# Wo ahead of the next PV, and the second norm's pieces at once, in every chunk that is needed next

## The chip, the cores and the metric

The kernel runs on one core of a Trainium2 chip. The metric is device time in microseconds, the median of several executions. A profile of one more execution shows each engine: TensorE (PE, with its weight loads PEld), VectorE (DVE), ScalarE (ACT), GpSimd (POOL) and SyncE (SP), which here only issues transfers.

## The reference, cut to what matters

A transformer block for 2048 positions of width 1024: a layer norm, attention of 32 query heads on one shared key and value head of width 32, a residual, a second layer norm, a gated feed-forward part of width 3584, and a second residual.

```python
q = heads(norm(x) @ wq); k = norm(x) @ wk; v = norm(x) @ wv
o = softmax(q @ k.T * Dh**-0.5) @ v
h = x + merge(o) @ wo
h2 = h + (sigmoid(norm(h) @ w_gate) * (norm(h) @ w_up)) @ w_down
```

## The kernel before

**Tiling.** The 2048 positions are cut into 8 chunks of 256 queries (c = 0 to 7), each of two tiles of 128 positions (tt = 0, 1). The 32 heads are 8 quads of four heads (q = 0 to 7). For one chunk and one quad, attention goes through the keys in 8 bursts. A burst of scores (`s_burst`, line 637) is eight small matmuls into PSUM tile S_ps, two exponentials on ScalarE follow (`one_exp`, line 660) and write the ring `Pr`, and later the PV group of the quad multiplies them with V (line 754). The row sums of the softmax are added in pairs on VectorE (`add_pair`, lines 694 and 703) and finished by a few matmuls (line 734) inside the PV group. When a PV group ends, VectorE copies the bank out (lines 772 and 773), takes the reciprocal (778, 780) and multiplies (784); that gives the quad's attention output in `QT`.

**After attention of a chunk.** `wo_group` (four a chunk: two tiles by two halves of the width, eight matmuls of 512 columns each, recorded at line 316) multiplies by Wo; line 844 adds x. `stats2` makes the second norm: statistics of each half (line 866), their merge (870), a square root and reciprocal by powers on GpSimd (342, 344), the norm itself (`ln_norm`, line 348); `transpose2` has SP transpose the tile by a transfer (line 487). Only then can the chunk's feed-forward part begin: 14 pairs of gate and up groups (line 932, 16 matmuls of 256 columns each, with a tanh at 951 and a product at 971), then four down groups (line 996, 28 matmuls of 512 columns each), each ended by an add on VectorE (1006) and a store by SP.

**What sets the order.** The order of all instructions on all engines is made when the program is built, by a loop near the end of the function that keeps a clock for each engine with a cost for each instruction. TensorE has two PSUM banks (X_ps) for everything but scores; a group holds one from its first matmul until VectorE or ScalarE has emptied it. At each step the loop does the first of these that it can: a score burst, if ScalarE has freed its place and the ring has room (`ring_need`, line 605: the next burst needs the exponentials of nine bursts before to have been read by PV); an item of the open PV group, or, while its exponentials or sums are not there, of the current other group; an item of a group that is marked `first`; a new PV group, if all its bursts and one more have been issued; else an item of the current group, or a new group. `next_group` takes a Wo group if one is ready, else the head of `ffn_list`, where the groups of gate, up and down stand in the order of the chunks. A gate group is only taken once both transposes of its chunk have landed by the clocks.

A Wo group is marked `first` in chunk 0 alone. There its four groups run through before a new PV group is opened, and the statistics are issued directly behind each add. In the other chunks the pieces of the second norm are put at the end of `lo`, the list of VectorE work that fills the time up to the next dated instruction, behind the pair sums that stand there.

With `first` unset, a PV group that becomes ready is opened between two Wo groups.

Of the kernel before, what the change touches and what calls it, by code (L numbers as in the profile page):

```python
# [52 lines left out]
def when(*ticks):  # L53

    return max([0.0] + [t[0].time(t[1]) + 0.05 for t in ticks if t is not None])


def need(eng, *ticks):
    clk = CLK[id(eng)]
    for t in ticks:  # L60
        if t is not None and t[0].emit is not None and t[1] > t[0].n:
            t[0].emit(t[1])
    clk[0] = max(clk[0], when(*ticks))
    for t in ticks:
        if t is not None:
            t[0].wait(eng, t[1])
# [18 lines left out]
def bass_sequential_preLN__grouped_kv_mqa__glu_gated_glu__prompt_kernel(  # L85
# [18 lines left out]
    NQ = D // P  # L104
    QC = 256
    NQC = S // QC
    TPQ = QC // P
# [7 lines left out]
    RP = 18  # L115
    HR = 5
    NGU = 4
    G_SUM, NPB, NO_SUM = 3, 4, (NQ,)
    HG = 3
    WD_AT, WD_GAP, WD_LATE = 6, 6, 6  # L120
# [5 lines left out]
    with ExitStack() as es:  # L126
        EC = es.enter_context

        def sb(name, shape, dt=BF16):
            return EC(nc.sbuf_tensor(name, [P] + shape, dt))  # L130
# [9 lines left out]
        hact_flat = sb("hact", [NFT * QC])  # L140
        gu = sb("gu", [NGU, 512], F32)
        wgu = sb("wgu", [4, DT, 256])
# [78 lines left out]
        def _(unused):  # L221
# [108 lines left out]
            def ln_mean(i):  # L330
                return c_pool.inc(pool.tensor_copy(out=mean[:, i:i + 1], in_=mv[:, i:i + 1, 0]), 0.2)  # L331
# [384 lines left out]
            def pv_group(g):  # L716
                c, q = g // NQ, g % NQ
# [51 lines left out]
                def evac(bank, tick):  # L769
                    force("a", lambda: g < 1 or g - 1 in ols_read)  # L770
                    need(dve, tick, ols_read.get(g - 1))
                    dve.tensor_copy(out=ols[:, 0:QC], in_=bank[:, 0:QC])  # L772
                    free = c_dve.inc(dve.transpose(ols[:, QC:2 * QC], bank[:, QC:2 * QC]), 0.7, 0.08)  # L773
                    t_ = [None]

                    def recip():
                        need(dve, free)
                        r_ = c_dve.inc(dve.reciprocal(l8[:], ols[:, QC:2 * QC].rearrange("p (a b) -> p a b", b=32)[:, :, 0]), 0.23)
                        need(dve, r_)
                        t_[0] = c_dve.inc(dve.transpose(ols[:, QC:2 * QC], l8[:].unsqueeze(2).to_broadcast([P, QC // 32, 32])), 0.4)  # L780

                    def mult():
                        need(dve, t_[0])
                        ot_val[(c, q)] = ols_read[g] = c_dve.inc(dve.tensor_tensor(
                            out=QT[:, q, c * QC:(c + 1) * QC], in0=ols[:, 0:QC], in1=ols[:, QC:2 * QC],
                            op=ALU.mult), 0.4)
                    if g == NQ - 1:
                        force("a", lambda: not any(x[0] == "a" for x in lo))
                        recip()
                        mult()  # L790
                    else:
                        put("a", 0.65, recip, lambda: when(free))
                        put("a", 0.4, mult, lambda: when(t_[0]))
                    return free
# [5 lines left out]
            def put(chain, cost, fn, ready, first=False):  # L800
                n = 0 if first else len(lo)
                while n < len(lo) and lo[n][0][0] == "l":
                    n += 1
                lo.insert(n, (chain, cost, fn, ready))
# [17 lines left out]
            def force(chain, done):  # L822
                while not done():
                    if lo[0][0][0] == "l":
                        t = lo[0][3]()
                        if t is not None and t <= k_dve[0] + 0.1:
                            lo.pop(0)[2]()
                            continue
                    i = [j for j, x in enumerate(lo) if x[0] == chain][0]
                    lo.pop(i)[2]()  # L830
# [7 lines left out]
            def wo_group(c, tt, dc):  # L838
                t = c * TPQ + tt

                def evac(bank, tick):
                    need(dve, tick, hx_val[t])
                    hv = hx[:, t % HR, dc * 512:(dc + 1) * 512]
                    h_val[t] = c_dve.inc(dve.tensor_tensor(out=hv, in0=bank, in1=hv, op=ALU.add), 0.61, 0.08)  # L844
                    stats2(c, tt, dc)
                    if dc == DC - 1:
                        h_done.add(t)
                    return h_val[t]
                items = mm_list([(QT[:, q, c * QC + tt * P:c * QC + (tt + 1) * P], wo[:, q, dc * 512:(dc + 1) * 512])
                                 for q in range(NQ)], lambda bank: bank, 512)  # L850
                g = _Group(items, evac, [wo_val[0]] + [ot_val[(c, q)] for q in range(NQ)])
                g.first = c == 0
                return g

            ln2_pow = {}

            def stats2(c, tt, dc):
                t, first = c * TPQ + tt, c == 0
                idx = NT + t
                src = hx[:, t % HR, :]  # L860
                chain = "l%d" % (t % 2)
                h_tick = h_val[t]

                def part(cc):
                    need(dve, h_tick)
                    ins = dve.bn_stats(st[:, idx % 4, cc, :], src[:, cc * 512:(cc + 1) * 512])  # L866
                    k_dve[0] += 0.64
                    if cc == DC - 1:
                        need(dve, c_dve.inc(ins))
                        st2_val[t] = c_dve.inc(dve.bn_aggr(mv[:, idx, :], st[:, idx % 4, :, :]), 0.2)  # L870
                        if first:
                            need(dve, st2_val[t])
                            v = c_dve.inc(dve.tensor_scalar(out=vz[:, idx:idx + 1], in0=mv[:, idx:idx + 1, 1], scalar1=EPS_B,
                                                            scalar2=None, op0=ALU.add), 0.1)
                            ln2_pow[t] = ln_pow(idx, v)
                            ln_mean(idx)
                            ln2_pow[t] = (c_pool, c_pool.n)
                        else:
                            ln2_pow[t] = ln_rstd(idx, st2_val[t])

                def norm():
                    before = hn_read[t - TPQ] if c > 0 else xnT_read[NT - TPQ + tt]
                    hn_val[t] = ln_norm(src, hn[:, tt, :], idx, st2_val[t], ln2_pow[t], before)
                    transpose2(c, tt)
                if first:
                    part(dc)
                else:
                    put(chain, 0.85 if dc else 0.64, lambda: part(dc), lambda: when(h_tick))
                if dc == DC - 1:
                    put(chain, 0.5, norm, lambda: None if t not in ln2_pow or c > 0 and t - TPQ not in hn_read else  # L890
                        when(ln2_pow[t]), first)
# [52 lines left out]
            def gate_group(c, fp):  # L944
                n = c * NFP + fp
                slot = gu[:, n % NGU, :]

                def evac(bank, tick):
                    def tanh():
                        need(act, tick, gu_read.get(n - NGU))  # L950
                        tanh_val[n] = c_act.inc(act.activation(out=slot, in_=bank, func=ACTF.Tanh, scale=0.5), T_TANH, 0.1)  # L951

                    def free(must):
                        if must:
                            while n not in tanh_val:
                                act_one(act_next()[1])
                        return (tanh_val[n] if must else when(tanh_val[n]) if n in tanh_val else
                                max(k_act[0], when(tick)) + T_TANH + 0.2)
                    act_work.append((tick, tanh, lambda: when(tick, gu_read.get(n - NGU))))
                    return free  # L960
                return _Group(half_group(c, fp, 0, None, ()).items, evac, [hnT_val[c * TPQ + i] for i in range(TPQ)])

            def up_group(c, fp):
                n = c * NFP + fp
                slot = gu[:, n % NGU, :]

# [54 lines left out]
            q_list = collections.deque()  # L1021
            wo_list = collections.deque((c, tt, dc) for c in range(NQC) for tt in range(TPQ) for dc in range(DC))
            ffn_list = collections.deque()
# [7 lines left out]
            cur, pv = [None], [None]  # L1031

            def busy(g):
                return g is not None and bool(g.items)

            def wo_ready():
                if not wo_list:
                    return False
                c, tt, dc = wo_list[0]
                t = c * TPQ + tt  # L1040
                return t in hx_val and when(hx_val[t]) <= k_pe[0] and all(
                    (c, q) in ot_val and when(ot_val[(c, q)]) <= k_pe[0] for q in range(NQ))
# [85 lines left out]
            for p in range(1, BPG):  # L1128
# [11 lines left out]
                q = p + 2  # L1140
# [45 lines left out]
            while True:  # L1186
# [41 lines left out]
                if starved and busy(cur[0]):  # L1228
                    run_item(cur[0])
                    continue  # L1230
                if not busy(cur[0]) and wo_list and wo_list[0][0] == 0 and wo_ready():
                    cur[0] = next_group()
                if busy(cur[0]) and cur[0].first:
                    run_item(cur[0])
# [61 lines left out]
```

## Time and profile before

| | us |
|---|---|
| median of 3 runs (1132.32 to 1133.71) | 1132.54 |
| the profiled execution | 1132.68 |
| its span, first to last instruction | 1130.9 |
| TensorE busy | 1090.1 |
| ScalarE busy | 1006.6 |
| VectorE busy | 860.1 |

The page gives the busy time of each engine, then slices of a fortieth of the span whose digits are tenths busy. A timeline row gives start, duration, engine, line, operation, tile written and read, and in brackets the idle time just before and what ended it. A stage row gives the stretch, its length, and for each engine the busy time with the number of instructions in brackets, then the granted TensorE clock, the share of the DMA engines and GB/s. A few per cent of the matmul records are missing from the trace; the weight loads are all there (3584 of gate and up, 896 of down, 256 of Wo), so counts are taken from them.

### The profile page before, as it was taken

How to read it: one execution, taken by the hardware profiler on the slowest of the kernel's cores; microseconds unless marked ns; L12 is line 12 of the kernel's file. 1: busy time of each engine (PE TensorE's matmuls, PEld its weight loads, DVE VectorE, ACT ScalarE, POOL GpSimd, SP SyncE). 2: the span in 40 equal slices, each digit the busy share in tenths (PEclk: the TensorE clock that was granted, in tenths of full speed). 3: DMA queues.
4: the chain of work that ended last, by engine and by line, in shares of the span. 5: the costliest groups of instructions: out<-in, count | busy, mean ns of one | idle time of the engine just before them, and what ended most of it. 6: DMA issues, size and time to landing. Idle time of an engine off the chain costs nothing.

```text
span 1130.9 us, 33101 instructions
## 1 busy us (share of the span) xinstructions
PE 1090.1 (96%) x14332; PEld 660.1 (58%) x14395; DVE 860.1 (76%) x1538; ACT 1006.6 (89%) x1150; POOL 67.4 (6%) x142
## 2 busy tenths in 40 slices
PE   7999999999899999999899999999899989999998
PEld 5663447754476545764477545764377535775784
DVE  7769977778878798788887798878887788884111
ACT  6999999999999999999999999999999999990110
POOL 4410010000100000000000010000100010001000
PEclk9999999999999999999999999999999999999999
DMA  8834117860366415661266514662167522769600
GB/s 196 176 81 171 39 39 220 231 187 24 88 187 191 118 29 150 192 191 47 61 194 195 147 31 134 193 192 57 34 185 213 160 39 62 209 193 263 180 1 19
DMA packets 282065, 150.38 MB, mean 133 GB/s; under 512 B 38592, under 2 KB 276160, under 8 KB 281920
## 3 DMA queue, kind: packets, MB, share of 16 engines
q1 hardware_dynamic: 274144, 137.65, 45.2%
q0 software_dynamic: 2544, 9.44, 2.4%
q8 instruction: 113, 1.85, 0.7%
q10 hardware_dynamic: 5232, 1.18, 0.7%
q14 instruction: 32, 0.26, 0.1%
HBM read 136.18 MB, written 4.19 MB: 124 GB/s over the span
## 4 chain that ended last, share of the span: by engine, by line
PE 71%; ACT 11%; DVE 11%; issue 4%; POOL 2%; DMA 1%; DVEq 0%; ACTq 0%
PE X_ps L932 34%; PE X_ps L996 12%; PE S_ps L637 10%; ACT Pr L660 9%; PE X_ps L754 8%; PE X_ps L316 5%; DVE pairs L694 3%; DVE pairs L703 3%; PE X_ps L734 1%; DVE st L866 1%; ACT hact L660 1%; POOL sd L342 1%; DVE hx L844 1%; POOL rs L344 1%; ACT QT L660 0%
## 5 line engine op out<-in xcount | busy, mean ns | idle before, releaser
L660 ACT ACTIVATE Pr<-S_ps 128x1024 bf16<-128x1024 f32 x992 | 931.8, 1137 | 8.8 <-PE S_ps L637 8.6
L694 DVE TENSOR_TENSOR pairs<-Pr 128x1024 bf16<-128x1024 bf16 x480 | 324.9, 684 | 76.6 <-ACT Pr L660 74.4
L932 PE MATMUL X_ps<-QT,wgu 128*128 128x256 bf16 x2096 | 267.3, 274 | 0.9 <-DVE ols L773 0.7
L703 DVE TENSOR_TENSOR pairs<-pairs 128x1024 bf16<-128x1024 bf16 x360 | 248.0, 689 | 22.3 <-DVE pairs L694 0.5
L932 PEld LDWEIGHTS X_ps<-QT,wgu 128*128 128x128 bf16 x2096 | 191.7, 98 | 58.3 <-issue 34.9
L996 PE MATMUL X_ps<-zone,hact 128*128 128x512 bf16 x849 | 206.6, 380 | 11.4 <-issue 4.9
L637 PE MATMUL S_ps<-QT,kT 32*128 32x256 bf16 x4096 | 204.4, 274 | 13.5 <-ACT Pr L660 7.0
L932 PE MATMUL X_ps<-QT 128*128 128x256 bf16 x1312 | 167.0, 273 | 0.2 <-DVE ols L773 0.2
L637 PEld LDWEIGHTS S_ps<-QT,kT 32*128 32x128 bf16 x4096 | 61.2, 92 | 156.9 <-ACT Pr L660 122.9
L754 PE MATMUL X_ps<-Pr,V 128*32 128x256 bf16 x3968 | 140.7, 275 | 4.0 <-DVE ols L773 1.5
L951 ACT ACTIVATE gu<-X_ps 128x512 f32<-128x512 f32 x112 | 74.4, 665 | 76.9 <-PE X_ps L932 75.9
L996 PEld LDWEIGHTS X_ps<-zone,hact 128*128 128x128 bf16 x896 | 78.4, 97 | 110.1 <-issue 25.2
L932 PEld LDWEIGHTS X_ps<-QT 128*128 128x128 bf16 x1312 | 121.8, 98 | 31.5 <-issue 17.1
L971 DVE SCALAR_TENSOR_TENSOR hact<-gu,X_ps 128x512 bf16<-128x512 f32 x112 | 76.5, 683 | 66.8 <-PE X_ps L932 65.8
L754 PEld LDWEIGHTS X_ps<-Pr,V 128*32 128x32 bf16 x3968 | 98.2, 97 | 30.3 <-issue 17.2
L316 PE MATMUL X_ps<-zone 128*128 128x256 bf16 (+2 forms) x512 | 77.1, 290 | 3.4 <-issue 2.4
L316 PE MATMUL X_ps<-wo,QT 128*128 128x512 bf16 x240 | 59.4, 380 | 1.8 <-issue 1.6
L331 POOL CAST mean<-mv 128x1 f32<-128x1 bf16 x28 | 9.9, 353 | 789.4 <-DVE mv L870 778.5
L316 PEld LDWEIGHTS X_ps<-zone 128*128 128x128 bf16 x512 | 36.7, 97 | 33.2 <-issue 16.7
L1006 DVE SCALAR_TENSOR_TENSOR hx<-X_ps,hx 128x512 bf16<-128x512 f32 x32 | 21.9, 684 | 42.2 <-PE X_ps L996 42.1
L772 DVE COPY ols<-X_ps 128x256 f32<-128x256 f32 x64 | 27.0, 421 | 16.0 <-PE X_ps L734 13.6
L316 PEld LDWEIGHTS X_ps<-wo,QT 128*128 128x128 bf16 x256 | 22.0, 98 | 29.2 <-issue 8.6
(76 smaller groups left out, 473.5 us busy)
## 6 DMA issues: line engine op xcount, KB each, us to landing
wgu<-in_B_w_gate_dram SPq DMA_DIRECT2D x73, 512.0 KB, 4.8
wgu<-in_B_w_up_dram SPq DMA_DIRECT2D x58, 512.0 KB, 4.8
QT<-in_B_w_up_dram SPq DMA_DIRECT2D x49, 512.0 KB, 4.9
QT<-in_B_w_gate_dram SPq DMA_DIRECT2D x33, 512.0 KB, 4.8
zone<-in_B_w_down_dram POOLq DMA_DIRECT2D x14, 512.0 KB, 5.4
hx<-in_A_x_dram SPq DMA_DIRECT2D x16, 256.0 KB, 3.5
out_dram<-hx SPq DMA_DIRECT2D x32, 128.0 KB, 1.7
Pr<-in_B_w_gate_dram SPq DMA_DIRECT2D x5, 512.0 KB, 7.9
```

The source lines that it names most:

```text
L316: ins = pe.matmul(sel(bank), lhsT=a, rhs=b, start=(i == 0), stop=(i == last))
L637: ins = pe.matmul(S_ps[:, bank, kt * QC:(kt + 1) * QC], lhsT=kT4[DH * j:DH * (j + 1), (2 * b + kt) * P:(2 * b + kt + 1) * P], rhs=QT[DH * ...
L660: c_e.inc(act.activation(out=p_tile(k, n % 2), in_=S_ps[:, 2 * pr:2 * pr + 2, :].rearrange("p a (b q) -> p (a b) q", q=QC), func=ACTF.Exp, ...
L694: add_half[k] = slot_use[slot] = c_dve.inc(dve.tensor_tensor(out=pairs[:, slot, :].rearrange("p (j q) -> p j q", j=4), in0=p4[:, :, 0, :], ...
L703: slot_use[x] = slot_use[y] = c_dve.inc(dve.tensor_tensor(out=pairs[:, x, :], in0=pairs[:, x, :], in1=pairs[:, y, :], op=ALU.add), T_ADD, ...
L754: ins = pe.matmul(bank[DH * j:DH * (j + 1), 0:QC], lhsT=V[:, 2 * b + kt, :], rhs=rhs(j), start=first and is_sum, stop=last and not is_sum, ...
L772: dve.tensor_copy(out=ols[:, 0:QC], in_=bank[:, 0:QC])
L932: ins = pe.matmul(bank[:, j * QC:(j + 1) * QC], lhsT=halves[i][:, dt, j * P:(j + 1) * P], rhs=QT[:, dt, c * QC:(c + 1) * QC], start=(dt == ...
L951: tanh_val[n] = c_act.inc(act.activation(out=slot, in_=bank, func=ACTF.Tanh, scale=0.5), T_TANH, 0.1)
L971: hact_val[(c, 2 * fp + 1)] = gu_read[n] = c_dve.inc(dve.scalar_tensor_tensor(out=hact[:, 2 * fp:2 * fp + 2, :], in0=slot.rearrange("p (a ...
L996: ins = pe.matmul(bank, lhsT=hact[:, ft, tt * P:(tt + 1) * P], rhs=wd[:, ft, dc * 512:(dc + 1) * 512], start=(ft == 0), stop=(ft == NFT - 1))
L1006: v = c_dve.inc(dve.scalar_tensor_tensor(out=hv, in0=bank, scalar=0.5, in1=hv, op0=ALU.mult, op1=ALU.add), 0.61, 0.08)
```

## The change

A function `urgent(c)` says whether chunk c is needed next: no query group is left to do, at most NEAR = 1 down group stands at the head of `ffn_list`, and what follows it belongs to chunk c. It takes the place of, or is added to, the test for chunk 0 in four spots: the mark `first` of a Wo group, the way the second norm's pieces are issued, the loop's choice of a Wo group ahead of a new PV group, and the reciprocal and product behind the last quad's PV, which are then issued at once.

```diff
+    NEAR = 1
...
-                    if g == NQ - 1:
+                    if g == NQ - 1 or q == NQ - 1 and urgent(c):
                         force("a", lambda: not any(x[0] == "a" for x in lo))
                         recip()
                         mult()
...
-                g.first = c == 0
+                g.first = c == 0 or urgent(c)
...
+            def urgent(c):
+
+                downs = 0
+                while downs < len(ffn_list) and ffn_list[downs][0] == "down":
+                    downs += 1
+                return not q_list and downs <= NEAR and downs < len(ffn_list) and ffn_list[downs][1] == c
+
             def stats2(c, tt, dc):
-                t, first = c * TPQ + tt, c == 0
+                t, first = c * TPQ + tt, c == 0 or urgent(c)
...
-                if not busy(cur[0]) and wo_list and wo_list[0][0] == 0 and wo_ready():
+                if not busy(cur[0]) and wo_list and (wo_list[0][0] == 0 or urgent(wo_list[0][0])) and wo_ready():
                     cur[0] = next_group()
                 if busy(cur[0]) and cur[0].first:
                     run_item(cur[0])
```

In `stats2`, `first` means: each statistic is issued with the add in front of it, the addition of the epsilon is done by VectorE (line 873) in place of GpSimd, GpSimd copies the mean last, and the norm is put at the head of `lo`.

## The prediction

> **What bounds the kernel now.** I read the page first: busy shares, then the slices.
>
> ```profile
> PE 1090.1 (96%) x14332; PEld 660.1 (58%) x14395; DVE 860.1 (76%) x1538; ACT 1006.6 (89%) x1150; POOL 67.4 (6%) x142
> PE   7999999999899999999899999999899989999998
> ACT  6999999999999999999999999999999999990110
> ```
>
> ScalarE is full up to slice 36 and nearly idle in the last four; TensorE is full everywhere. So there are two stages: attention, where the exponentials fill ScalarE and feed-forward work fills TensorE's spare time, and a tail that is TensorE alone. The timeline's last sums of PV and then the chain that ended last show the tail.
>
> ```profile
> 1019.13 0.29 PE L734 MATMUL X_ps<-pairs,ones 128*32 128x256 bf16 x4
> ...
> 1022.29 6.85 PE X_ps L316 x31
> 1031.37 10.74 PE X_ps L996 x49
> 1055.06 48.91 PE X_ps L932 x448
> ```
>
> PV ends at 1019.4; then come Wo of chunk 7, the four down groups of chunk 6, all of chunk 7's gate and up; its downs follow from 1104.0 to the end. 49 matmuls in 10.74 us are 219 ns each with nothing between. TensorE's work is the same in both kernels. So as long as work waits for it, the time moves only with TensorE's idle or slowed time. I looked for that with the busy time by stage: first the boundary stages (Wo of chunks 1, 2, 3, 5, 6), with one stretch between boundaries.
>
> ```profile
> 262.00:304.00 42.00, 38.28 (x496) 16.93 (x500) 37.13 (x68) 40.68 (x46) 3.93 (x8) 0.96 0.16 36
> 304.00:386.00 82.00, 80.96 (x1143) 55.01 (x1143) 66.01 (x115) 81.96 (x96) 0.00 (x0) 1.00 0.67 188
> 386.00:436.00 50.00, 47.14 (x610) 21.67 (x608) 42.88 (x77) 50.00 (x56) 3.96 (x8) 1.00 0.15 38
> 505.00:566.00 61.00, 56.74 (x717) 26.57 (x725) 51.63 (x91) 58.54 (x66) 4.04 (x8) 1.00 0.23 62
> 757.00:826.00 69.00, 64.96 (x813) 31.92 (x822) 59.71 (x106) 68.81 (x77) 4.03 (x8) 1.00 0.27 73
> 884.00:952.00 68.00, 63.64 (x788) 31.15 (x799) 57.85 (x102) 65.92 (x75) 4.18 (x8) 0.97 0.30 69
> ```
>
> The columns are length, TensorE, its weight loads, VectorE, ScalarE, GpSimd, granted clock. TensorE lacks 3.7, 2.9, 4.3, 4.0 and 4.4 us in the boundaries, and 1.0 us in 82 between them. Part of that is not real: where fewer matmuls than loads are listed, a record is missing. The timeline gives the real gaps, in brackets.
>
> ```profile
> 294.48 0.40 PE L637 MATMUL S_ps<-QT,kT 32*128 32x256 bf16 x8 [0.43 <-ACT Pr L660]
> 296.31 0.40 PE L637 MATMUL S_ps<-QT,kT 32*128 32x256 bf16 x8 [1.44 <-ACT Pr L660]
> 297.77 0.29 PE L734 MATMUL X_ps<-pairs,ones 128*32 128x256 bf16 x4 [1.06 <-DVE pairs L703]
> 429.71 0.40 PE L637 MATMUL S_ps<-QT,kT 32*128 32x256 bf16 x8 [1.44 <-ACT Pr L660]
> 549.56 0.39 PE L996 MATMUL X_ps<-zone,hact 128*128 128x512 bf16 x1 [2.65 <-DVE hx L1006]
> 806.24 0.82 PE L996 MATMUL X_ps<-zone,hact 128*128 128x512 bf16 x3 [1.24 <-DVE ols L773]
> 926.38 0.39 PE L996 MATMUL X_ps<-zone,hact 128*128 128x512 bf16 x1 [2.14 <-DVE hx L1006]
> ```
>
> Chunk 1 loses 0.43 + 1.44 + 1.06 = 2.9 us, chunk 2 1.4, chunk 3 2.7, chunk 5 1.2, chunk 6 2.1. Behind two of them the granted clock drops (the column before the last two).
>
> ```profile
> 298.80:302.20 3.40, 3.40 (x37) 1.46 (x30) 2.95 (x7) 2.24 (x4) 0.00 (x0) 0.50 0.06 17
> 926.90:930.30 3.40, 2.93 (x56) 1.63 (x49) 2.70 (x7) 1.94 (x2) 0.00 (x0) 0.50 0.38 110
> ```
>
> Half speed for 3.4 us, busy 3.40 and 2.93: 1.7 and 1.5 us more lost. In all 13.5 us at boundaries.
>
> The Trainium skill, "TensorE: Matmul & The Clock Gate", "What's actually happening", says the clock halves after an idle window of about 3.4 us. The trace is stricter or looser by place: the 2.14 us gap was followed by a drop, the 2.65 us gap was not. By the page alone no gap here is long enough, the 3.2 us would stay, and the sum below would end 3.2 us higher at most; it does not decide the sign.
>
> **The change part by part.** What happens in chunk 1 is the plainest case. Line 844 adds the last Wo group to x, 866 and 348 are its statistics and norm; first chunk 1, then chunk 0, where the pieces already go in at once.
>
> ```profile
> 285.42 0.67 DVE L844 TENSOR_TENSOR hx<-X_ps,hx 128x512 bf16<-128x512 f32 x1
> 291.11 0.69 DVE L866 BATCH_NORM_STATS2 st<-hx 128x6 f32<-128x512 bf16 x1
> 294.44 0.55 DVE L348 TENSOR_SCALAR hn<-hx,mean,rs 128x1024 bf16<-128x1024 bf16 x1 [0.50 <-DVE pairs L694]
> 299.85 1.67 PE L932 MATMUL X_ps<-QT,wgu 128*128 128x256 bf16 x7
> ```
> ```profile
> 154.14 0.69 DVE L844 TENSOR_TENSOR hx<-X_ps,hx 128x512 bf16<-128x512 f32 x1 [0.73 <-PE X_ps L316]
> 157.43 0.55 DVE L348 TENSOR_SCALAR hn<-hx,mean,rs 128x1024 bf16<-128x1024 bf16 x1 [0.62 <-POOL mean L331]
> ```
>
> *Statistics at once.* From the add to the norm take 9.0 us in chunk 1 and 3.3 in chunk 0: 5.7 us less. Nothing is added but a small VectorE instruction in place of a GpSimd one (both in the 3.3). The transpose that SP issues behind the norm, and the first gate, come 5.4 us after the norm (294.44 to 299.85). That transpose moves ahead of an output store on SP's queue, which nobody waits for soon; GpSimd does nothing else at the time (8 instructions in the whole stage).
>
> *Wo ahead of PV.* Which chunks does the condition meet? The stages from the end of Wo to the next gate, restricted to down matmuls, say how many groups of 28 were still to do (the count of loads, second bracket):
>
> ```profile
> 284.35:299.80 15.45, 6.67 (x27) 2.41 (x28) 0.97 0.31 62
> 416.20:430.00 13.80, 6.63 (x26) 2.32 (x28) 1.00 0.21 39
> 537.20:559.20 22.00, 12.88 (x51) 4.63 (x55) 1.00 0.19 42
> 665.80:684.70 18.90, 12.90 (x52) 4.66 (x56) 1.00 0.23 50
> 914.20:948.50 34.30, 19.36 (x77) 7.04 (x83) 0.95 0.21 32
> 1028.70:1054.60 25.90, 23.71 (x108) 10.93 (x112) 1.00 1.00 221
> ```
>
> One group in chunks 1 and 2, two in 3 and 4 (chunk 5 lies between them and 6), three in 6, four in 7. NEAR = 1 therefore meets chunks 1 and 2 as they stand. But feed-forward work that is done earlier in chunk 1 shortens every later queue, by 28 matmuls for each 6.0 us saved, so I expect chunks 3 to 6 to be met, some of the time.
>
> What does PV's delay cost? First the page's group of exponentials, then three rows of chunk 1:
>
> ```profile
> L660 ACT ACTIVATE Pr<-S_ps 128x1024 bf16<-128x1024 f32 x992 | 931.8, 1137 | 8.8 <-PE S_ps L637 8.6
> ...
> 279.27 0.62 PE L754 MATMUL X_ps<-Pr,V 128*32 128x256 bf16 x16
> 279.82 0.40 PE L637 MATMUL S_ps<-QT,kT 32*128 32x256 bf16 x8
> 283.12 0.59 PE L316 MATMUL X_ps<-wo,QT 128*128 128x512 bf16 x2 [0.16 <-issue]
> ```
>
> The score burst at 279.82 may only go once the first burst of PV's group has been read (the ring, line 605). Some eight Wo matmuls were left at 279.27: 8 x 0.22 (6.85 / 31) = 1.8 us. With Wo first the burst goes at about 281.4, 1.6 us later. An exponential takes 931.8 / 992 = 0.94 us and the burst 0.40, so ScalarE had about 0.5 us in hand (an estimate) and idles 1.1 us. TensorE computes Wo meanwhile, so I cost this at nothing: what hides it is the reserve in the tail, 112 down matmuls (23.7 us) that are done in the held time instead. Without that cover each held microsecond costs one.
>
> So chunk 1: last Wo at 280.9 in place of 284.6, norm at 281 + 3.3 = 284.4, gate from 289.8. The last down group with PV and scores fills TensorE until about 291. Its 2.9 us of gaps go, and the slow clock with them: 4.6 us. Chunk 2 is the same kind (waiting for the norm with the downs used up): 1.4 us. In chunks 3, 5 and 6 the releaser is VectorE emptying a bank late, because it stood waiting for a norm or worked its backlog. Earlier statistics move that backlog, not all of it away, and the condition may not be met: between 0 and 2.65 + 1.24 + 2.14 + 1.5 = 7.5 us, I take half, 3.7. The forced reciprocal and product after quad 7's PV bring nothing in chunk 1 and at most 1 us elsewhere, hidden by the down group in flight: nothing.
>
> New idle time: VectorE now waits for GpSimd's power between Wo's evacuations (0.62 us in chunk 0's row), and behind the waiting norm stand the pair sums, for which PV's sum matmuls wait; and the last norm of chunk 7 is covered by fewer downs. No row shows it. From below 0; from above 0.6 us for each of six chunks and 3 us at the end: 6.6. Chunk 0's Wo, the nearest, ran without a gap, so I take 1.5.
>
> **Sum:** 4.6 + 1.4 + 3.7 - 1.5 = 8.2 us. The profiled execution has a span of 1130.9 and a time of 1132.68, 0.14 over the median. 1132.5 - 8.2 gives **1124.3 us**.
>
> **The rivals.** *Slower: the exponentials are held too long.* In chunk 2 PV started at once after a score burst, before any Wo:
>
> ```profile
> 404.81 1.06 PE L754 MATMUL X_ps<-Pr,V 128*32 128x256 bf16 x32
> 405.90 0.40 PE L637 MATMUL S_ps<-QT,kT 32*128 32x256 bf16 x8
> ```
>
> Four Wo groups ahead (6.85 us) would put the burst of 405.90 at 412.2, and ScalarE would idle 5.8 us. Six such chunks are 35 us; less the 1.3 + 2.5 + 2.1 = 5.9 us that ScalarE idles now in the stages of chunks 1, 3 and 6, attention ends 29 us later than about 1019.4. Then the reserve is used up and TensorE waits: 1048.4 + 2.5 (last PV to Wo) + 6.9 (Wo) + 9 (3.3 and 5.4 to the gate) + 48.9 + 26.9 = 1142.6, a time of about 1144. It decides from where attention ends 17 us later, a hold of 3.8 us a chunk. For it: ScalarE's full row. Against it: held time brings feed-forward work forward, so the next Wo starts earlier and collides less.
>
> The Trainium skill, "Perfetto Trace Analysis", "Identifying the Most-Contended Engine", says that matmul busy time is no good measure and weight-load busy time is better. By that (58% against ScalarE's 89%) ScalarE would be the bound and this rival the forecast; the back-to-back 219 ns above speak for TensorE.
>
> *Only the first chunks.* If the condition meets chunks 1 and 2 alone: 4.6 + 1.4 - 0.5 = 5.5 us, 1127.
>
> *Moved, not removed.* Pair sums come later by the statistics put before them (four of 0.69 us a chunk), PV keeps its bank longer, and about the same gaps return there: 1132. For it: three of the five gaps end at VectorE.
>
> **How the numbers follow.** Chances: forecast 0.50 (1119 to 1127), first chunks only 0.15, moved 0.16, slower 0.19. This kernel's measurement can tell about 0.2%, 2.3 us, from no change. Faster by more: 0.50 + 0.15 + 0.03 of "moved" = 0.68. Within: 0.09 of it. Slower: 0.19 + 0.04 = 0.23. The range goes from all 13.5 us saved with a little to spare, 1117, to 1136, which leaves out most of the slower rival.
>
> **What would show it.** Right: in the changed profile the last statistics of chunk 1 stand next to the last add, the norm starts near 284 to 285, no TensorE gap over 1 us lies between 284 and 300, and the clock stays full there; fewer than four down groups stand in the tail. Wrong: ScalarE gaps of more than 4 us at each Wo, downs in the tail gone and a wait of several us between Wo and gate of chunk 7 (the slower rival); gaps released by lines 703, 773 or 1006 of the old size just after PV (moved); chunks 3 to 6 with two or more downs behind Wo (first chunks only).

## The result, and the profile after

The changed kernel takes 1127.00 us (median of 6 runs, 1125.80 to 1129.92) against 1132.77 for the kernel before beside it (6 runs, 1131.68 to 1134.80): a ratio of 0.9949 [0.9935, 0.9964]. That is faster by 0.5%, 5.8 us, where 8.2 were forecast. The profiled execution has a span of 1125.1 us against 1130.9. Single executions differ by up to 2.4 us already in chunk 0, where the order is the same in all of them: its PV row after a wait of 0.97 or 0.98 us starts at 169.44 before, at 168.47 after, and between 167.97 and 170.32 in the runs below. So starts of two executions are compared by their distance from that row. Lines behind the new function have moved by one, and by eight from the statistics on: scores are now line 638, exponentials 661, the add of x 845, statistics 874, norm 349, gate and up 940, down 1004.

First the page of the changed kernel, busy time and slices:

```profile
PE 1091.8 (97%) x14336; PEld 659.3 (59%) x14395; DVE 865.7 (77%) x1552; ACT 1006.7 (89%) x1150; POOL 63.2 (6%) x128
...
PE   7899999999999999999999999999999999999798
ACT  6999999999999999999999999999999999992110
```

The four 8s of TensorE that stood between slices 11 and 33 are gone. A new 7 stands in slice 38, past the end of attention. The work is the same. So something was won at the boundaries and something lost in the tail. The boundary stages, with the columns of the table of before:

```profile
262.00:304.00 42.00, 40.88 (x536) 20.32 (x540) 38.16 (x71) 40.90 (x47) 3.49 (x6) 1.00 0.25 65
386.00:436.00 50.00, 48.67 (x617) 25.38 (x621) 45.13 (x82) 48.43 (x56) 3.42 (x6) 1.00 0.31 81
505.00:566.00 61.00, 59.51 (x766) 30.62 (x774) 53.07 (x95) 59.43 (x68) 3.41 (x6) 1.00 0.30 83
757.00:826.00 69.00, 67.51 (x850) 36.34 (x855) 60.50 (x109) 67.43 (x77) 3.42 (x6) 1.00 0.33 92
884.00:952.00 68.00, 66.51 (x845) 35.80 (x850) 59.60 (x108) 66.43 (x76) 3.42 (x6) 1.00 0.32 88
```

The clock is 1.00 in all five, and TensorE lacks 1.1 to 1.5 us where it lacked 2.9 to 4.4. More of the same stage's work is done: 540 weight loads in chunk 1's stage for 500, 850 in chunk 6's for 799. The brackets of the timeline, added up from 85 us to the end of attention for all idle times over 0.2 us, give 16.65 us before and 5.42 after. None after is over 0.97 us, none ends at VectorE any more, and the two stretches at half clock (1.7 and 1.5 us) are gone too. What a boundary of chunks 2 to 6 still has is one gap of 0.25 or 0.26 us and one like this, in which a gate group waits for ScalarE's tanh:

```profile
421.46 0.28 PE L940 MATMUL X_ps<-QT 128*128 128x256 bf16 x1 [0.55 <-ACT gu L959]
```

So the stretch up to the end of attention, its boundaries above all, gave 11.2 + 3.2 = **14.4 us**.

Chunk 1 in the timeline of the changed kernel, row by row as it was forecast:

```profile
277.33 2.76 PE L317 MATMUL X_ps<-wo,QT 128*128 128x512 bf16 x11
280.33 0.68 DVE L845 TENSOR_TENSOR hx<-X_ps,hx 128x512 bf16<-128x512 f32 x1
280.36 0.40 PE L638 MATMUL S_ps<-QT,kT 32*128 32x256 bf16 x8
280.80 13.87 ACT L661 ACTIVATE Pr<-S_ps 128x1024 bf16<-128x1024 f32 x15 [1.10 <-PE S_ps L638]
281.05 0.69 DVE L874 BATCH_NORM_STATS2 st<-hx 128x6 f32<-128x512 bf16 x1
284.25 0.55 DVE L349 TENSOR_SCALAR hn<-hx,mean,rs 128x1024 bf16<-128x1024 bf16 x1
291.01 0.27 PE L940 MATMUL X_ps<-QT,wgu 128*128 128x256 bf16 x1
```

Wo runs through; the score burst goes behind it and ScalarE stands for 1.10 us; the last statistics follow the last add at once; the norm comes 3.9 us after the add, where it took 9.0; the gate follows without a gap of TensorE. The time that ScalarE stands at Wo is called its hold from here on; two later rows show it in chunks 2 and 6:

```profile
407.04 13.88 ACT L661 ACTIVATE Pr<-S_ps 128x1024 bf16<-128x1024 f32 x15 [1.57 <-PE S_ps L638]
...
912.07 13.87 ACT L661 ACTIVATE Pr<-S_ps 128x1024 bf16<-128x1024 f32 x15 [1.57 <-PE S_ps L638]
```

From 407.04 to 912.07 are four periods of 126.26 us: the chunks have become copies of one another. The stages from the end of Wo to the next gate, restricted to down matmuls, say the same (chunks 1, 2, 6 and 7; loads in the second bracket):

```profile
279.65:290.90 11.25, 6.36 (x26) 2.32 (x28) 1.00 0.26 48
405.90:417.00 11.10, 6.16 (x26) 2.33 (x28) 1.00 0.30 49
910.90:922.00 11.10, 6.13 (x26) 2.33 (x28) 1.00 0.26 49
1033.50:1047.00 13.50, 5.99 (x27) 2.72 (x28) 0.90 1.21 237
```

One group of 28 stands behind Wo in every chunk, where there had been one, one, two, two, two, three and four. The last row is the price: in chunk 7 one group instead of four covers the last norm. The tail in the timeline (SPq and ACTq are the queues of SP and ScalarE; their durations are those of the issue; nine loads stand between the first SPq row and the second, both counted):

```profile
1024.27 0.37 SPq L226 DMA_DIRECT2D Pr<-in_B_w_gate_dram  x1
...
1026.86 7.07 PE L317 MATMUL X_ps<-wo,QT 128*128 128x512 bf16 x32
1033.98 5.99 PE L1004 MATMUL X_ps<-zone,hact 128*128 128x512 bf16 x27
1034.37 5.48 ACTq L488 DMA_TRANSPOSE QT<-hn  x2
1036.42 1.68 SPq L226 DMA_DIRECT2D Pr<-in_B_w_gate_dram  x1
1037.53 0.55 DVE L349 TENSOR_SCALAR hn<-hx,mean,rs 128x1024 bf16<-128x1024 bf16 x1 [1.43 <-POOL mean L332]
1047.15 3.57 PE L940 MATMUL X_ps<-QT,wgu 128*128 128x256 bf16 x16 [7.18 <-issue]
```

The norm is done at 1038.1, but the gate comes 9.1 us later. The chain that ended last names what lay between:

```profile
1034.37 7.00 DMA QT<-hn
1041.37 5.78 issue
1047.15 50.98 PE X_ps L940 x448
```

It shows the first transpose; the 5.78 us of "issue" are the wait for the second, as the DMA issues below let one see: two transposes on ScalarE's queue with a median of 8.0 us from issue to landing, so one of 7.0 and one of about 9, against 3.1 for the fourteen on SP's queue.

```profile
QT<-hn SPq DMA_TRANSPOSE x14, 3.1
...
QT<-hn ACTq DMA_TRANSPOSE x2, 8.0
```

In the kernel before the same two were as slow, under 112 down matmuls:

```profile
QT<-hn ACTq DMA_TRANSPOSE x2, 7.8
```

And the 448 gate and up matmuls take 50.98 us where they took 48.91; the clock falls in the idle time:

```profile
1044.30:1051.20 6.90, 4.05 (x20) 2.94 (x21) 0.00 (x0) 0.44 (x1) 0.00 (x0) 0.51 0.43 71
```

So the tail loses 7.18 + 2.07 = **9.25 us**. The balance is 14.4 - 9.25 = 5.2 us saved. The spans differ by 5.8, of which 1.0 stands already at the row of chunk 0 (169.44 and 168.47), so by 4.8 from there on.

### The profile page after: what moved, and what is told of

Read it like the earlier page. It is cut to its first block, busy times and chain, and to the rows that moved or that the text cites. A ratio compares the mean times of both kernels' runs of the same rounds, so it can differ in the third digit from the quotient of the medians.

```text
span 1125.1 us, 33112 instructions
## 1 busy us (share of the span) xinstructions
PE 1091.8 (97%) x14336; PEld 659.3 (59%) x14395; DVE 865.7 (77%) x1552; ACT 1006.7 (89%) x1150; POOL 63.2 (6%) x128
## 4 chain that ended last, share of the span: by engine, by line
PE 83%; ACT 11%; issue 3%; DMA 1%; DVE 1%; POOL 0%; DVEq 0%
PE X_ps L940 37%; PE X_ps L1004 14%; PE S_ps L638 13%; PE X_ps L755 9%; ACT Pr L661 9%; PE X_ps L317 8%; PE X_ps L735 1%; ACT hact L661 1%; PE X_ps L422 1%; DMA QT<-hn 1%; ACT QT L661 0%; ACT gu L959 0%; ACT wo L661 0%; DMA zone<-hn 0%; ACT kT L511 0%
## 5 line engine op out<-in xcount | busy, mean ns | idle before, releaser
L940 PE MATMUL X_ps<-QT 128*128 128x256 bf16 x1328 | 171.5, 274 | 2.2 <-ACT gu L959 2.2
L959 ACT ACTIVATE gu<-X_ps 128x512 f32<-128x512 f32 x112 | 72.0, 642 | 68.6 <-PE X_ps L940 68.4
L755 PEld LDWEIGHTS X_ps<-Pr,V 128*32 128x32 bf16 x3968 | 95.8, 96 | 30.1 <-issue 19.8
L343 POOL TENSOR_TENSOR sd<-vz,powers 128x1 bf16<-128x1 bf16 x32 | 24.1, 754 | 821.5 <-DVE vz L881 810.7
```

The source lines that it names most:

```text
L343: t_ = c_pool.inc(pool.tensor_tensor(out=sd[:, i:i + 1], in0=vz[:, i:i + 1], in1=half[:, 0:1], op=ALU.pow), 0.6)
L755: ins = pe.matmul(bank[DH * j:DH * (j + 1), 0:QC], lhsT=V[:, 2 * b + kt, :], rhs=rhs(j), start=first and is_sum, stop=last and not is_sum, ...
L940: ins = pe.matmul(bank[:, j * QC:(j + 1) * QC], lhsT=halves[i][:, dt, j * P:(j + 1) * P], rhs=QT[:, dt, c * QC:(c + 1) * QC], start=(dt == ...
```

## The experiments

The theory behind the first runs: the place of Wo and the early statistics save together, by ending the waits at the boundaries, and the tail gives back 9 us because the last two transposes land late beside nine weight loads. The rivals: one of the two parts does it alone; the tail's wait is the last norm's own length, whatever the loads do; and ScalarE's hold of 1.1 to 1.6 us costs time.

### One part alone

**Early statistics without Wo's place** (e1_stats_only), the changed kernel with:

```diff
-                    if g == NQ - 1 or q == NQ - 1 and urgent(c):
+                    if g == NQ - 1:
...
-                g.first = c == 0 or urgent(c)
+                g.first = c == 0
...
-                if not busy(cur[0]) and wo_list and (wo_list[0][0] == 0 or urgent(wo_list[0][0])) and wo_ready():
+                if not busy(cur[0]) and wo_list and wo_list[0][0] == 0 and wo_ready():
```

> The changed kernel with the second norm's pieces at once in the chunk that is needed next, but Wo not marked first and not chosen ahead of PV there, and without the forced reciprocal. Theory (the time follows TensorE's gaps at the chunk boundaries, most of which come from the late norm): the gaps of chunks 1 and 2 that end at the norm go, those at VectorE half; 1127 to 1130 us, ScalarE never held. Rival (Wo ahead of PV is what moves the time): 1131 to 1133 us.

Measured: 1131.95 us, 0.9987 [0.9978, 0.9995]. The two largest waits in its timeline:

```profile
555.23 0.37 PE L940 MATMUL X_ps<-QT,wgu 128*128 128x256 bf16 x1 [3.91 <-DVE ols L774]
...
677.21 0.39 PE L1004 MATMUL X_ps<-zone,hact 128*128 128x512 bf16 x1 [1.86 <-DVE hx L1014]
```

The larger waits that are left end at VectorE's emptying of banks: 1.00 and 1.49 us in chunks 1 and 2, chunk 3's wait grown from 2.65 to 3.91, a new one in chunk 4. The clock still drops behind the last two (from 555.2 and from 678.1). That is what "moved, not removed" had said of the whole change; of this part alone it is true. My theory's 1127 to 1130 us was too good; the rival's 1131 to 1133 held.

**Wo's place without early statistics** (e2_wo_only), the changed kernel with:

```diff
-                    if g == NQ - 1 or q == NQ - 1 and urgent(c):
+                    if g == NQ - 1:
...
-                t, first = c * TPQ + tt, c == 0 or urgent(c)
+                t, first = c * TPQ + tt, c == 0
```

> The changed kernel with Wo first and ahead of PV in the chunk that is needed next, but the norm's pieces put at the end of VectorE's list as before, and without the forced reciprocal. Theory: the last Wo ends 4 to 12 us earlier in each chunk, but the norm follows it by 9 us in place of 3.3 and one down group (6 us of matmuls) does not cover that: gaps of 1 to 3 us stay at each boundary; 1128 to 1133 us. Rival (Wo's place is what moves the time): 1125 to 1128 us, no gap over 1 us between Wo and gate.

Measured: 1128.97 us, 0.996 [0.9947, 0.9974]. No idle time at a boundary is over 1.06 us and one down group stands behind Wo in every chunk, as in the whole change. So the place of Wo makes the regular order. The time lies in my theory's range, but the rows are nearer to the rival's, which had no gap over 1 us. Its tail waits less than the whole change's; the last norm and the last load's issue:

```profile
1037.57 2.80 SPq L226 DMA_DIRECT2D Pr<-in_B_w_gate_dram  x1
1041.89 0.55 DVE L349 TENSOR_SCALAR hn<-hx,mean,rs 128x1024 bf16<-128x1024 bf16 x1 [1.81 <-POOL rs L345]
...
1048.75 1.65 PE L940 MATMUL X_ps<-QT,wgu 128*128 128x256 bf16 x7 [5.28 <-issue]
```

The norm ends 2.1 us after the last load was issued (1042.4 and 1040.4), where in the whole change both are at 1038.1, and the gate follows 6.3 us later instead of 9.1: the loads have gone on meanwhile. So the difference of the two ratios (0.996 and 0.9949, 1.2 us, with intervals that overlap) may understate what the statistics bring; e10 below takes them out where the tail does not blur it.

### The tail

**The nine weight loads behind the last transposes** (e3_late_weights), in the changed kernel:

```diff
@@ transpose2
                                                      tt, hn_val[t], *before)
+                if last and tt == TPQ - 1:
+                    assert pr_ticks
+                    for i in range(H_PR, len(halves) - 1):
+                        half_free.append((i, pr_ticks + [hnT_val[t]]))
+                    load_halves()
...
@@ the end of the last PV group
                         pr_given[0] = True
-                        for i in range(H_PR, len(halves) - 1):
-                            half_free.append((i, [(c_pv, c_pv.n), (c_dve, c_dve.n)]))
-                        load_halves()
+                        pr_ticks.extend([(c_pv, c_pv.n), (c_dve, c_dve.n)])
```

> The changed kernel, but the nine weight loads into the freed ring wait until the last chunk's transposes have landed. Theory (the 7.2 us wait before chunk 7's first gate comes from transposes that stand behind nine loads of 512 KB in the DMA engines, and costs 2 us more by the half clock after it): the second transpose lands about 3 us after its issue in place of 9, the gap shrinks to 1 to 2 us, no half clock, no wait for weights; 1119 to 1121 us. Rival (the wait is the chain of norm, power and transpose itself, which two down groups' worth of cover would have hidden): gap still 5 to 7 us, 1126 to 1128 us, or more where the late weights are waited for.

Measured: 1119.07 us, 0.9876 [0.9861, 0.989]. Timeline, then DMA issues, then the chain:

```profile
1041.79 0.39 SPq L226 DMA_DIRECT2D Pr<-in_B_w_gate_dram  x1
1041.80 1.91 PE L945 MATMUL X_ps<-QT,wgu 128*128 128x256 bf16 x16 [1.28 <-issue]
```
```profile
QT<-hn ACTq DMA_TRANSPOSE x2, 3.1
```
```profile
1041.80 49.07 PE X_ps L945 x448
```

The transposes, still on ScalarE's queue, take 3.1 us, the gate waits 1.28 us instead of 7.18, the clock stays at 1.00, and gate and up take 49.07 us. On every engine but SP the order of the instructions is that of the changed kernel. So all but 1.28 us of the tail's wait was the loads, not the length of the norm nor the queue. In what way the loads hold the transposes up, the rows do not show. No order in this study is faster beyond the scatter: 1.2% below the kernel before. Repeated later on another chip (e3_again), as the base for more edits:

> The changed kernel with the late weight loads once more, to stand on the same chip beside the next three: 1118 to 1121 us.

Measured: 1120.41 us, 0.9882 [0.9867, 0.9896].

**The same edit in the kernel before** (e4_before_late_weights; diff as above):

> The kernel before with the same late weight loads. Theory: the transposes land earlier, but four down groups (24 us) covered them already: 1132 to 1133.5 us, no difference. Rival (the loads' place in the queue matters by itself): more than 3 us faster or slower.

Measured: 1133.62 us, 1.0 [0.9992, 1.0009]. Its two transposes take 3.2 us and the time is the same. So the slow transposes had cost nothing before: the four down groups hid them. The change exposed them.

**The idle time filled** (e8_fill): the changed kernel with matmuls on weights at hand, into idle score banks, ahead of chunk 7's first gate; no one reads what they write.

```diff
                             ffn_list.popleft()
+                            if a == ("g", NQC - 1, 0):
+                                for i in range(30):
+                                    pe.matmul(S_ps[:, i % 6, :], lhsT=wo[:, 0, 0:P], rhs=wo[:, 0, 0:512], start=True, stop=True)
+                                    k_pe[0] += 0.2176
                             return (up_group if a[0] == "u" else gate_group)(c, a[2])
```

> The changed kernel with 30 matmuls of 512 columns into idle score banks ahead of chunk 7's first gate group; their results are not used. They fill 6.5 us of the 7.2 us wait. Theory (the wait costs 7 us, and the half clock behind it 2 more): the clock stays full, gate and up take 48.9 us in place of 51.0, 1124.5 to 1125.5 us. Rival (the clock drop costs nothing, or is not caused by the idle time): no difference, 1126.5 to 1127.5 us, or slower by the added work.

Measured: 1125.88 us, 0.9932 [0.9919, 0.9946], where e5 beside it, whose order is the changed kernel's (below), had 1127.47. The chain:

```profile
1041.93 4.75 PE S_ps L1072 x22
...
1048.40 48.91 PE X_ps L940 x448
```

Gate and up are back at 48.91 us, the number of before, with the clock at 1.00. The added matmuls delay nothing: the gate starts 6.47 us behind the last down group (1041.93 to 1048.40) where the changed kernel's wait was 7.18 (the transposes land sooner in this execution, with a median of 7.3 us). That the row reads 1048.40 and not 1047.15 comes from chunk 0, from which on this execution stands 1.6 us later (170.06 and 168.47). So the rows say 2.07 + 0.7 = 2.8 us saved; the times say 1.6, between the two ranges expected, and their intervals overlap. The rows show that the 2.07 us are the clock's; the total is too small a difference to show more.

### The threshold

**NEAR = 2** (e5_near2) and **NEAR = 0** (e6_near0), one number in the changed kernel, here for the first:

```diff
-    NEAR = 1
+    NEAR = 2
```

> The changed kernel with NEAR = 2: two down groups may still stand ahead. Theory (what the changed kernel lacks is only cover for chunk 7's transposes, since a single down group is left there): Wo starts earlier against its down groups, one or two of them stay behind it, and in chunk 7 the 7.2 us wait is covered by a second group of 6 us: 1118 to 1122 us. Rival (one group left is no accident but what the time needs): 1126 to 1130 us.

Measured: 1127.47 us, 0.9946 [0.9931, 0.996]. My expectation of a second down group left over fell; the rival's range held. The order of the instructions is that of NEAR = 1 on every engine, with one group behind Wo and a wait of 7.16 us in the tail. So a threshold of two decides nothing that one does not; a larger one was not tried.

> The changed kernel with NEAR = 0: the rule holds only once all downs of the chunk before have been begun. Theory: Wo is then first only when nothing is left behind it, so either it is not met and the gaps of before stay, or it is met and the norm and transpose are waited for with nothing to do, 4 to 8 us a chunk: 1130 to 1145 us. Rival (the number in the rule does not matter, only that Wo is marked): 1125 to 1128 us.

Measured: 1133.36 us, 1.0006 [0.9997, 1.0015]. The order of the instructions is that of the kernel before on every engine: the condition is never met, as the theory had allowed, and the waits of before are back, such as chunk 2's:

```profile
428.27 0.40 PE L638 MATMUL S_ps<-QT,kT 32*128 32x256 bf16 x8 [1.43 <-ACT Pr L661]
```

### ScalarE's hold

**Eight small chained copies on ScalarE behind the last PV of chunks 1 to 6** (e7_act_extra; with the late loads of e3, so that the tail does not blur it; the copies go to a spare column):

```diff
+                    if q == NQ - 1 and 0 < c < NQC - 1:
+                        need(act, const_val)
+                        for i in range(8):
+                            need(act, spare_val[0])
+                            spare_val[0] = c_act.inc(act.activation(out=spare, in_=ones[:, 0:4], func=ACTF.Copy), 0.23)
```

> The changed kernel with the late weight loads, and eight small chained copies on ScalarE behind the last PV of chunks 1 to 6, 2 to 4 us of ScalarE a chunk. It tells whether the exponentials that Wo holds back cost time. Theory (TensorE is the bound, ScalarE's hold of 1.1 to 1.6 us a chunk is free): the holds shrink by what is added, the end of attention moves by the rest, and the time by less than half of what is added: 1119 to 1126 us for 12 to 24 us added. Rival (ScalarE is the bound): the time grows by all that is added, 1131 us or more.

Measured: 1147.03 us, 1.0119 [1.0103, 1.0135]. Against e3's ratio that is 0.024, some 27 us, for 10.8 us of copies (48 of 225 ns). The theory fell; the time lies in the rival's range, but not by its reason, which was that the time grows by what is added. First the downs between Wo and gate in chunks 1 and 3 (the row of 540 to 550 starts behind chunk 3's Wo), then chunk 3's rows of ScalarE and TensorE, then the last sums of PV.

```profile
281.70:292.50 10.80, 6.42 (x25) 2.23 (x27) 1.00 0.27 50
540.10:550.20 10.10, 0.00 (x0) 0.00 (x0) 0.90 0.39 80
```
```profile
541.28 9.27 ACT L663 ACTIVATE Pr<-S_ps 128x1024 bf16<-128x1024 f32 x10 [4.03 <-PE S_ps L640]
...
549.69 0.61 PE L640 MATMUL S_ps<-QT,kT 32*128 32x256 bf16 x8 [1.44 <-ACT Pr L663]
...
1052.49 0.28 PE L737 MATMUL X_ps<-pairs,ones 128*32 128x256 bf16 x4
```

From chunk 3 to chunk 6 no down group is left behind Wo. ScalarE then stands 4.03 to 4.13 us at Wo in each of these chunks, TensorE has nothing but scores and PV until the norm and the transposes are through, and the clock falls. A period takes 131.8 to 135.1 us in place of 126.26. Attention ends at 1052.8; in the changed kernel's timeline it ends at 1022.2 (its last such row starts at 1021.88), 29 us earlier by the row of chunk 0 (170.32 and 168.47). That is the picture of the prediction's slower rival: the cover used up, ScalarE idle for more than 4 us at Wo, a time near its 1144. Its sum is not met term by term. It had an end 29 us later from holds of 5.8 us in six chunks; here the holds are shorter and in four, the copies and further waits add to them, and the cover is gone in chunks 3 to 6, while chunk 7 still has a group of 28. The edge is real; the change stands on the near side of it.

**Three copies** (e11_act_small; the same edit with `range(3)`):

> The changed kernel with the late weight loads and three small chained copies on ScalarE behind the last PV of chunks 1 to 6, 0.7 us a chunk, 4.1 in all, less than the hold of 1.1 to 1.6 us. Theory (the hold is slack: what ScalarE gets below it is free, what it gets beyond uses up the last down group): 0 to 1 us slower. Rival (every microsecond of ScalarE costs one or more): 4 us slower or more.

Measured: 1118.95 us, 0.9872 [0.9859, 0.9886], beside e3_again's 0.9882: nothing, for 4.4 us of copies. The page's group and chunk 2's hold:

```profile
L794 ACT ACTIVATE powers<-ones 128x4 bf16<-128x4 bf16 x18 | 4.4, 242 | 0.4
```
```profile
408.10 13.88 ACT L663 ACTIVATE Pr<-S_ps 128x1024 bf16<-128x1024 f32 x15 [0.89 <-PE S_ps L640]
```

The hold shrinks from 1.57 to 0.89 us and takes the copies in; the period stays at 126.26 us (the next hold ends at 534.36). So what ScalarE does inside the hold is free: ScalarE does not set the period here. Between three and eight copies a chunk, 0.7 and 1.8 us of ScalarE, lies the edge.

### The smaller parts, with the tail's wait gone

**The forced reciprocal and product left out** (e9_no_force; e3 with):

```diff
-                    if g == NQ - 1 or q == NQ - 1 and urgent(c):
+                    if g == NQ - 1:
```

> The changed kernel with the late weight loads, without the forced reciprocal and product behind the last quad's PV. Theory: they bring nothing, since a down group is in flight while they wait: within 1 us of the kernel with the force. Rival: Wo becomes ready later and its chunk's hold of ScalarE grows, 2 to 6 us slower.

Measured: 1119.23 us, 0.9873 [0.986, 0.9887], beside 0.9882 for e3_again. It brings nothing: the order of the instructions is that of e3 on every engine, so the force decides nothing in it.

**The early statistics left out** (e10_no_stats; e3 with):

```diff
-                t, first = c * TPQ + tt, c == 0 or urgent(c)
+                t, first = c * TPQ + tt, c == 0
```

> The changed kernel with the late weight loads, with the second norm's pieces put at the end of VectorE's list as before. The statistics' own part, with Wo ahead and without the wait for weights. Theory: with one down group behind Wo the later norm is nearly covered, gaps of about 1 us a chunk: 2 to 4 us slower. Rival (the statistics at once are needed as much as Wo's place): 6 us slower or more.

Measured: 1124.27 us, 0.9917 [0.9903, 0.993], 0.0035 above e3_again: 4.0 us, the upper end of what the theory had. Its idle times over 0.2 us, from 85 us to the last gate, add up to 9.2 us, e3's to 5.4 and, in the repeat, 6.7. Part of it stands at the last gate, which waits longer for the later norm than e3's 1.28 us; in the profiled execution, the slowest of the five, the clock drops behind it and gate and up take 50.73 us in place of 49.07:

```profile
1046.24 2.43 PE L945 MATMUL X_ps<-QT,wgu 128*128 128x256 bf16 x16 [2.14 <-issue]
```
```profile
1046.24 50.73 PE X_ps L945 x448
```

So with the tail mended the early statistics bring 4 us, and the rest comes from Wo's place. Without that place they bring 1.5 (0.0013, e1). By the medians the two do not simply add, but the intervals (0.0005 to 0.0022 in e1, each ratio here with one about 0.0028 wide) are too wide to be sure.

## Why the prediction was right or wrong

The sign, the range and the mechanism at the boundaries held; 1127.0 stands 2.7 us above the 1124.3. Two terms were mis-sized: one had 4.7 us too little saved, the other 7.75 us too little lost. That the time still came so near is in part luck, since they went against each other.

**Chunk 1: right, nearly to the row.** Forecast were the last Wo at 280.9, the norm at 284.4, the gate not before 289.8 with TensorE busy until about 291, and a hold of 1.1 us on ScalarE. Measured: Wo's last row ends at 280.1, the norm starts at 284.25, the gate at 291.01, a hold of 1.10, in an execution that stands 1.0 us earlier from chunk 0 on. Of the 4.6 us 4.2 came; a wait of 0.43 us for ScalarE's tanh is new.

**Chunk 2: right.** Its wait of 1.4 us is gone; all its gaps over 0.2 us fell from 1.9 to 0.8.

**Chunks 3, 5 and 6: half of 7.5 us was too little; 8.1 came** (gaps of 9.1 us fell to 2.4, and 1.5 us of slow clock went). The argument was that VectorE's backlog moves and that the condition may be met some of the time only. Wo runs through in every chunk from 1 to 6, with 28 down matmuls behind it each time and no gap that ends at VectorE. That VectorE's emptying of Wo's banks no longer meets PV's is the likely reason; no run isolates it. e1 shows that the early statistics alone leave waits of this kind (3.91, 1.86 and 1.25 us); e2 shows that Wo's place alone takes them away. The prediction gave the statistics 5.7 us of chunk 1's argument and left Wo's place mostly as a cost: the weight was the wrong way round. All together, with 0.9 us elsewhere, gave 14.4 us against 9.7 forecast (4.6 + 1.4 + 3.7).

**The term that failed: "new idle time", taken as 1.5 us with an upper bound of 3 us at the end.** It cost 9.25 us, all in the tail. Even the term's whole upper bound of 6.6 did not hold it. The prediction saw that chunk 7's norm is "covered by fewer downs" but said that no row shows the price; the only time from norm to gate that it works out is chunk 1's 5.4 us. Chunk 7 is no such chunk: its transposes go through ScalarE's queue while SP's nine loads are under way, and its gate comes 9.6 us after the norm's start (1037.53 to 1047.15). The row was in the profile of before: 7.8 us on one queue and 3.1 on the other. e3 shows that the loads are the cause, e4 that they cost nothing before, e8 that 2.07 us of the loss are the clock's.

**The forced product at nothing: right** (e9). **The held exponentials at nothing: not quite.** The cover was the one that the prediction named. The reserve fell from 112 matmuls to 28, that is by 18.4 us at 219 ns; of these, 14.4 us fill the former waits, and 3.7 us are the time by which attention ends later (853.7 us behind the row of chunk 0 in place of 850.0); 0.3 us are not accounted for. But the reserve was also what covered chunk 7's norm, so held time is paid back there once the cover is short. How much of the 9.25 us that is was not tried by itself. What e11 shows is that more work on ScalarE inside the hold is free.

**The rivals.** "First chunks only" gave the measured time, 1127, by luck: the rows of one down group in every chunk rule its reason out. "Moved" holds for the early statistics alone (e1). "Slower" did not come, but e7 reaches it with 1.8 us of copies a chunk (10.8 / 6) against a hold of 1.57, so it deserved its place.

**The page of the Trainium skill** named there, "Perfetto Trace Analysis", "Identifying the Most-Contended Engine", would have made ScalarE the bound by weight-load busy time; the share of peak arithmetic that it names beside it was not worked out here. e11 speaks against ScalarE as the bound of this order (4.4 us more on ScalarE, nothing lost) and e7 shows how little room there was (10.8 us more, 27 lost).

What stays open: why e7 costs quite 27 us is read from its rows, not tried part by part. Nor is it tried how the loads slow the transposes. How much of the tail's 7.18 us would remain with the transposes on SP's queue but the loads in place was not tried.

## What to carry to other kernels

When a change uses up work that lay behind a dependent step, look up what that work was hiding, at that very place: here a row of DMA issues, 7.8 us on one queue beside 3.1 on another, was free until its cover went. A bulk load that nobody needs yet is best held until the small transfer on the path has landed. And before a critical step is put ahead of another engine's feed, find the slack of that engine per period: here 1.57 us, where three copies were free and eight cost two and a half times their length.

## What the runs showed of the hardware

- A transpose by DMA that took 3.1 us took 7.0 and about 9 beside nine weight loads of another queue, while the core moved 237 GB/s (the stage row of 1033.50 above), and 3.1 again with the loads behind it (e3).
- Within and behind the 7.18 us of idle time TensorE's clock was at half from 1044.3 to 1051.2; TensorE was busy for 4.05 us of that. The Trainium skill, "TensorE: Matmul & The Clock Gate", "What's actually happening", gives windows of about 3.4 us; the 6.9 us here are two of them, and the trace agrees so far. In e7 the clock is at 0.51 from 548.4 to 562.1, 13.7 us or four of them. Short gaps do not follow that page's rule: in e4, whose order in attention is that of before, the clock halved behind chunk 3's gap of 2.65 us and not behind chunk 6's of 2.15, the other way round than in the kernel before; e6, with the same order once more, halved behind both. So the same gap may or may not cost. The stages of e4, the first behind chunk 3's gap, the second across chunk 6's:

```profile
550.70:554.10 3.40, 3.40 (x30) 1.04 (x19) 3.11 (x8) 2.79 (x4) 0.00 (x0) 0.50 0.17 60
926.50:930.30 3.80, 2.80 (x60) 1.58 (x61) 3.70 (x8) 3.15 (x5) 0.00 (x0) 1.00 0.49 106
```
